# A third of a projection's K as seven block products in an attention and two-stage gated kernel on one core

## The chip, the core and the metric

The kernel runs on one core of a Trainium2 chip. The metric is the device time of one execution in microseconds; of several runs the median counts. Five engines work from queues of their own: TensorE (PE; its weight loads are PEld), VectorE (DVE), ScalarE (ACT), GpSimd (POOL) and SyncE (SP). SP issues most of the transfers and GpSimd some.

## What is computed

Everything is float32. A windowed attention gives x, 2304 tokens by 512; x goes through a gated stage and a projection, and the result through a second gated stage without the nonlinearity, w3 and a last projection.

```python
attn_out = softmax_window_64(q, k, v)           # (4, 8, 576, 64)
x = attn_out.transpose(0, 2, 1, 3).reshape(2304, 512)
# first stage, w_gate and w_val (512, 1536), w_out (1536, 512)
g = x @ w_gate
h = (g * (1.0 / (1.0 + np.exp(-g)))) * (x @ w_val)
x2 = h @ w_out
# second stage, w1 and w2 (512, 1024), w3 (1024, 1024), w_out2 (1024, 512)
return ((x2 @ w1) * (x2 @ w2) @ w3) @ w_out2
```

## The kernel before

A float32 matrix product is done in words: each operand is split into a high word of reduced precision (a cast, L218, mostly on ScalarE) and a rest (the operand less its high word, L227, on VectorE), and three matmuls (high by high, high by rest, rest by high) make one product. A block product of 256 by 256 by 384 tokens is six matmuls where it has two slabs of K.

*Tiling.* The 2304 tokens lie in thirds (`tp`) of 768, each in two halves of 384 (`T`). The inner dimension of the first stage has six blocks `fp` of 256.

*Gated stages* (`gated`, matmuls at L687). A unit is one `fp`, one of the two matrices (`x` is 0 for w_gate, 1 for w_val) and one third. Its two-by-two block product is made as seven block products of six matmuls each (numbered 1 to 7; two slots of a unit's time grid belong to its neighbours). They go into four PSUM banks al, ga, be, de (with an a or b behind, for x 0 or 1). Product 1 goes to al; ScalarE copies al out (c11, L377), product 2 goes to ga, and VectorE adds ga to the copy (L699). `AT` is the grid: 1, 2, 5, 6, then those of other units between, 7, 4, 3. VectorE multiplies the two matrices' results to h (`put`, L709), and h goes to DRAM as two stores for each `fp` and third (L777), from SP's queue in the first stage and from GpSimd's in the second. 36 units make the first stage, 24 the second. In the last `fp` of the first stage the order of units was w_gate over all thirds, then w_val over all thirds.

*Projection* (`project`, L852). It takes a third of the tokens at a time. For each of 12 K slabs and 8 output banks (4 output blocks by 2 halves) three matmuls run: 864 in all. h comes back from DRAM by `Rows` (L811, one key being one `fp` and one half, 384 KB, named pl; ph is its high word). The words of w_out lie in 16 tiles of six 128 by 128 blocks (`Resident`, L1306), loaded from DRAM where `Split` put them earlier. The eight banks are copied out to X at the end of a third (L838 and the lines of copies).

*Preparing weights.* Blocks of weights are loaded into staging tiles st_* by SP (L263), turned into words on VectorE and ScalarE (L194 to L227) and, for w_out, w_out2 (z) and w3, written to DRAM (L1238, L1241). w3 is transposed on VectorE in 32 by 32 pieces into one of two tiles by_w (L1225), and each half of a block leaves by four stores of 32x16x32 elements (L1245), 64 in all, in runs of 128 bytes, from SP.

*What sets the order.* A planner in Python (`Plan`) puts the jobs of VectorE, ScalarE, GpSimd and the queues between the matmuls, by rank and due time, with estimated costs, free slots (`NSLOT` 56 tiles of 384 KB) and a count kept back (`keep`). `plan.need` forces a job that a matmul needs. Events at a unit or at a step of the projection start the making of weights and the loads. An SP transfer also waits for the one eight before it, since they share eight semaphores.

Of the kernel before, what the change touches and what calls it, by code (L numbers as in the profile page):

```python
# [35 lines left out]

@with_exitstack
def window_attention_moe_kernel(ctx: ExitStack, tc: tile.TileContext, q, k, v, w_gate, w_val, w_out, w1, w2, w3, w_out2, out):
# [13 lines left out]
    NSLOT = 56  # L52
# [5 lines left out]
    half = ctx.enter_context(tc.tile_pool(name="half", bufs=7))  # L58
# [27 lines left out]
    class Job:  # L86
        def __init__(self, fn, after=(), cost=None, lag=0.0, rank=0, slots=0, due=0.0, early=False):

            self.rank, self.slots, self.due, self.early = rank, slots, due, early
            self.fn, self.after, self.cost, self.lag, self.done = fn, [x for x in after if x], cost, lag, None  # L90

    class Plan:
        def __init__(self):
# [4 lines left out]

            self.slots, self.keep = NSLOT - ATTENTION, 0

        def job(self, fn, after=(), lag=LAG, slots=0, due=0.0, early=False, **cost):
            j = Job(fn, after, cost, lag, self.rank, slots, due, early)
# [14 lines left out]
        def emit(self, j, e):  # L117
# [4 lines left out]
            j.done = self.free[e] + j.lag  # L122

# [5 lines left out]
        def fill(self, but):  # L129
            limit = self.now + self.ahead  # L130
            while True:
                best = None
                for e, free in self.free.items():
# [3 lines left out]
                    for j in self.queue:  # L137
                        if e not in j.cost or (j.early and e == "DVE" and not self.early) or any(x.done is None for x in j.after):
                            continue
                        if j.slots and self.slots < j.slots + self.keep:  # L140
# [44 lines left out]
    def narrow(part, load, due):  # L185
# [7 lines left out]
        n = 512  # L193
# [17 lines left out]
    def cast(hi, src, after, n, slots=1, negate=False, due=0.0):  # L211
# [7 lines left out]
        return plan.job(fn, after, slots=slots, due=due, early=True, ACT=act(n), DVE=0.1 + 0.0006 * n,  # L219
# [18 lines left out]
    def loading(fn, after=(), slots=0, lag=9.0):  # L238
        return plan.job(fn, after, lag=lag, slots=slots, SP=0.5)
# [4 lines left out]
    class Doubles:  # L244
# [5 lines left out]
        def load(self):  # L250
# [13 lines left out]
            if self.second is None:  # L264
                self.loaded = [loading(lambda eng: part(eng, 0, 2), before, lag=plan.landing)] * 2
            else:
# [4 lines left out]
        def narrowed(self):  # L271
            return [narrow(lambda j=j: self.st[:, 512 * j:512 * j + 512], self.loaded[j], self.due) for j in range(2)]
# [4 lines left out]
    class Weights(Doubles):  # L277
# [3 lines left out]
        def __init__(self, w, n, name):  # L281
            super().__init__(w[:, 256 * n:256 * n + 256].rearrange("(c p) f -> p c f", p=P), name)
            self.ops, self.jobs, self.count, self.gone = {}, {}, 0, 0
# [13 lines left out]
        def make(self):  # L297
# [7 lines left out]
            for p in PRODUCTS:  # L305
                after, due = ready if p in sums else [ready[at[p][1] - 1]], self.due + AT[p]
# [346 lines left out]

    def gated(xop, left, order, func, hd, events, apart=0):
# [20 lines left out]
        class Unit:  # L675
# [26 lines left out]
            def put(self, i, t, src):  # L702

                h, direct = self.h(i, t), (i, t) == (1, 0)
                if self.x and direct:
# [8 lines left out]
                elif direct:  # L714
                    negated(h, src)
# [754 lines left out]
```

## Time and profile before

| | us |
|---|---|
| median of 3 runs | 824.29 |
| lowest and highest | 823.33 and 826.74 |
| the profiled execution | 825.91 |
| its span, by the profile | 824.2 |
| PE busy in it | 815.6 |
| projection, from its first matmul to its last | 149.99 |

The profile comes from one execution. Its engines' busy times and its timelines are in microseconds from the span's start; a row of a timeline has the start, the duration, the engine and line, the operation, and in brackets the idle time before it with what ended it. Two matmuls overlap, so a row of one says 0.33 while the next starts 0.17 later. Stages lie so: attention to about 107, first gated stage to 363, projection 363.35 to 513.34, second gated stage, w3 and the last projection.

### The profile page before, as it was taken

The numbers are of one execution on the slowest core, as the hardware profiler recorded it, in microseconds if no ns is written. First come the engines' busy times: TensorE is split into PE (matmuls) and PEld (weight loads), VectorE is DVE, ScalarE is ACT, GpSimd is POOL, SyncE is SP. The second block draws the span as 40 slices with busy tenths as digits, with TensorE's granted clock in tenths as the row PEclk, the third lists the DMA queues.
The fourth block names the chain that finished last, engine by engine and source line by source line (L and its number), as shares of the span: only waits on it lengthen the run. The fifth ranks groups of instructions, "written<-read, shape, count | busy, mean of one in ns | idle before, by whom it ended". The sixth has DMA issues, their size and how long they took to land.

```text
span 824.2 us, 15599 instructions
## 1 busy us (share of the span) xinstructions
PE 815.6 (99%) x5718; PEld 785.2 (95%) x5718; DVE 640.6 (78%) x1354; ACT 454.6 (55%) x1194; POOL 92.4 (11%) x135
## 2 busy tenths in 40 slices
PE   9999999999999999999999999999999999999998
PEld 6777899999999999999999999999999998899997
DVE  5999889686887939865888683877888844789994
ACT  7899987555555535633564551444444423755543
POOL 3666833000000000000000000000010100000000
PEclk9999999999999999999999999999999999999999
DMA  9989396253562344599996722024555289007632
GB/s 187 199 186 199 61 217 125 90 192 128 192 229 83 137 153 161 210 360 380 385 290 157 233 71 103 20 83 142 167 180 175 110 299 335 27 2 207 181 73 78
DMA packets 172766, 140.23 MB, mean 170 GB/s; under 512 B 120849, under 2 KB 142609, under 8 KB 171665
## 3 DMA queue, kind: packets, MB, share of 16 engines
q1 hardware_dynamic: 167888, 125.86, 50.8%
q0 software_dynamic: 4800, 13.37, 5.9%
q8 instruction: 45, 0.74, 0.4%
q14 instruction: 33, 0.26, 0.1%
HBM read 92.27 MB, written 42.99 MB: 164 GB/s over the span
## 4 chain that ended last, share of the span: by engine, by line
PE 90%; SPq 4%; DMA 2%; ACT 1%; DVE 1%; issue 1%; ACTq 0%
PE o L852 18%; PE ala L687 15%; PE alb L687 14%; PE bea L687 7%; PE beb L687 7%; PE acc L1010 5%; PE al L1153 4%; PE gaa L687 4%; PE gab L687 3%; SPq L403 2%; PE be L1153 2%; PE al L1085 2%; PE PV L519 2%; PE PT L499 2%; PE S L466 1%; PE T L429 1%
## 5 line engine op out<-in xcount | busy, mean ns | idle before, releaser
L852 PE MATMUL o<-ph,wo 128*128 128x384 f32 x576 | 146.4, 334 | 0.0
L852 PEld LDWEIGHTS o<-ph,wo 128*128 128x128 f32 x576 | 104.1, 188 | 0.0
L852 PE MATMUL o<-pl,wo 128*128 128x384 f32 x288 | 96.3, 334 | 0.0
L377 ACT ACTIVATE ha<-ala 128x384 f32<-128x384 f32 x102 | 49.6, 488 | 50.0 <-PE ala L687 49.3
L777 POOL DMA_DIRECT2D h<-ha x24 | 13.0, 546 | 548.2 <-DVE ha L709 548.2
L699 DVE TENSOR_TENSOR ha<-ha,bea 128x384 f32<-128x384 f32 x60 | 33.2, 553 | 38.3 <-PE bea L687 22.3
L852 PEld LDWEIGHTS o<-pl,wo 128*128 128x128 f32 x288 | 54.1, 188 | 0.3 <-DVE pl L227 0.3
L480 ACT ACTIVATE pexp<-S,stat 128x128 f32<-128x128 f32 x144 | 53.1, 421 | 0.0
L218 ACT CAST hf<-h 128x384 fp32r<-128x384 f32 x84 | 38.8, 513 | 14.5 <-DVE h L231 13.2
L712 ACT ACTIVATE ha<-ha 128x384 f32<-128x384 f32 x54 | 28.4, 526 | 33.1 <-DVE ha L699 33.1
L227 DVE TENSOR_TENSOR hf<-h,hf 128x384 fp32r<-128x384 f32 x84 | 42.3, 548 | 4.8 <-ACT hf L218 4.8
L227 DVE TENSOR_TENSOR pl<-pl,ph 128x768 fp32r<-128x768 f32 x36 | 33.4, 953 | 14.6 <-ACT ph L218 14.3
L218 ACT CAST ph<-pl 128x768 fp32r<-128x768 f32 x36 | 29.1, 839 | 26.2 <-DMA pl<-h 23.6
L490 POOL TENSOR_TENSOR pexp<-pexp,stat 128x384 f32<-128x384 f32 x48 | 39.1, 835 | 28.6 <-DVE stat L487 14.1
L377 ACT ACTIVATE c12b<-alb 128x384 f32<-128x384 f32 x30 | 14.8, 492 | 48.7 <-PE alb L687 48.6
L480 ACT ACTIVATION_READ_ACCUMULATOR pexp<-S,stat 128x1 f32 x144 | 37.2, 260 | 0.0
L699 DVE TENSOR_TENSOR c22b<-c22b,beb 128x384 f32<-128x384 f32 x30 | 16.6, 553 | 25.8 <-ACT c22b L377 25.8
L687 PE MATMUL ala<-xo,w_g_7h 128*128 128x384 f32 x120 | 30.4, 336 | 0.5 <-ACT ha L377 0.5
L687 PE MATMUL ala<-xo,w_g_1h 128*128 128x384 f32 x126 | 29.2, 335 | 0.0
L473 DVE TENSOR_REDUCE stat<-S 128x3 f32<-128x384 f32 x48 | 24.4, 550 | 4.8 <-PE S L466 4.4
L218 ACT CAST xp<-X 128x384 fp32r<-128x384 f32 x42 | 19.7, 520 | 10.5 <-DVE X L231 7.5
L377 ACT ACTIVATE c11b<-alb 128x384 f32<-128x384 f32 x30 | 14.7, 490 | 19.2 <-PE alb L687 19.2
(628 smaller groups left out, 2465.8 us busy)
## 6 DMA issues: line engine op xcount, KB each, us to landing
h<-ha SPq DMA_DIRECT2D x36, 384.0 KB, 3.0
pl<-h SPq DMA_DIRECT2D x36, 384.0 KB, 6.1
h<-ha POOLq DMA_DIRECT2D x24, 384.0 KB, 3.2
h<-h SPq DMA_DIRECT2D x24, 384.0 KB, 6.7
st_w<-in_moe_w_dram SPq DMA_DIRECT2D x8, 1024.0 KB, 6.2
st_wo<-in_moe_w_out_dram SPq DMA_DIRECT2D x6, 1024.0 KB, 5.5
wo<-by_wo SPq DMA_DIRECT2D x12, 512.0 KB, 4.0
st_g<-in_moe_w_gate_dram SPq DMA_DIRECT2D x5, 1024.0 KB, 6.4
```

Of the source, the lines that this page charges most:

```text
L218: (eng.copy if eng is nc.scalar else eng.tensor_copy)(out=hi(), in_=src())
L227: return plan.job(lambda eng: eng.tensor_tensor(out=lo(), in0=src(), in1=hi().bitcast(F32), op=ALU.subtract), after, slots=slots, due=due, ...
L377: nc.scalar.mul(out=out, in_=in_, mul=-1.0)
L473: nc.vector.tensor_reduce(out=st[:, 0, x, :], in_=sc[2 * m + x], op=ALU.max, axis=AX.X, negate=True)
L480: nc.scalar.activation(out=pe[:, jj, :], in_=so[:, jj, :], func=AF.Exp, bias=st[:, 0, x, jj:jj + 1], accum_out=st[:, 1, x, jj:jj + 1])
L490: nc.gpsimd.tensor_tensor(out=pe, in0=pe, in1=st[:, 3, x, :].unsqueeze(2).to_broadcast([P, SUB, P]), op=ALU.mult)
L687: nc.tensor.matmul(acc, lhsT=self.wt.ops[p, x][:, m, :], rhs=self.xs.ops[p, m][:, y, :], start=start and n == 0, stop=n == 5, skip_group_c ...
L699: nc.vector.tensor_tensor(out=out, in0=x, in1=y, op=ALU.add)
L712: nc.scalar.activation(out=h, in_=src, func=func, scale=-1.0 if direct else 1.0)
L852: nc.tensor.matmul(acc[m, x], lhsT=wos.tiles[i // 6][:, i % 6, :], rhs=rows[2 * tp + x].words(f, b), start=f == n == 0, stop=f == NF - 1 a ...
L1010: nc.tensor.matmul(acc, lhsT=w3T[i][c // 3][:, x, (c % 3) * P:(c % 3) * P + P], rhs=zt[c, y], start=c == k == 0, stop=c == NI - 1 and k == 2)
L1153: nc.tensor.matmul(acc, lhsT=right.ops[p, m, y][:, P * k:P * k + P], rhs=self.xs.ops[p, m][:, x, :], start=bool(name) and n == 0, stop=n = ...
```

## The change

*Seven products.* In the projection the blocks `fp` 0 and 1 (`SEVEN`, a third of K) are taken as two-by-two block products: halves of tokens by halves of the slab pairs, in seven products over both, in the order of `STEPS`. Each product runs for two output blocks m and two g (the two `fp`). Bank al is copied by ScalarE into ga (after product 1) and into de (after product 7), and later products accumulate there. The four other blocks are plain as before, but go bank by bank (al, be, ga, de). Evictions become copies and additions into X.

*Its operands.* h of these blocks is stored in the layout `h7d`, as seven parts (four transfers for two, 1.75 times the bytes), and twelve transfers from DRAM to DRAM with an addition, on GpSimd's queue, make the sums (`spread`). w_out's blocks 0 and 1 are made by class `Seven`: four sums and seven rests of 256 columns, stored in 14 pieces. Row keys per third go from 12 to 15, w_out's tiles from 16 to 20. Rows have slots of their own (`ROWS`).

*Seeded units.* From unit 6 on in both gated stages ScalarE copies al into bank ga, and product 2 accumulates on it. Product 2 changes places with product 5 (`AT_SEEDED`). VectorE's addition of ga is gone.

*Others.* The stores of w3 go by GpSimd's queue. The last `fp` of the first stage runs in the order that the second had (thirds first). Staging loads of w_out and w3 are made with the weights, with a due time; loads of w_out's tiles hang on events. `NSLOT` is 58, `half` has 5 buffers.

```diff
+AT_SEEDED = {1: 0, 5: 2, 2: 3, 6: 4, 7: 8, 4: 12, 3: 13}
-    NSLOT = 56
+    NSLOT = 58
-    half = ctx.enter_context(tc.tile_pool(name="half", bufs=7))
+    half = ctx.enter_context(tc.tile_pool(name="half", bufs=5))
...
+    SEEDED = 6
+    SEVEN = (0, 1)
...
+                elif (i, t) == (0, 0) and self.seeded:
+                    nc.scalar.copy(out=h, in_=src)
+                    plan.charge("ACT", act(T))
...
+                    self.seeded = self.n >= SEEDED
+                    if self.seeded:
+                        self.ga = bank(f"ga{self.name}")[:, :T]
+                    self.c11 = self.ga if self.seeded else self.own(0, 0, "c11")
                     later(1, lambda: self.copy(self.c11, self.al))
+                elif p == 2 and self.seeded:
+                    plan.wait(self.read)
+                    self.mm(self.ga, 2)
+                    self.put(0, 0, self.ga)
...
+    H_AT = {1: 0, 7: 1, 2: 2, 3: 3, 4: 4, 6: 5, 5: 6}
+    def spread(fp, tp, h):
+        to, f = h7d[tp], SEVEN.index(fp)
+        (h0, h1) = (t.rearrange("p (c t) -> p c t", c=2) for t in h)
+        for at, src in (((0, 2), h0), ((2, 4), h1), ((4, 6), h1), ((6, 7), h0[:, :1])):
+            nc.sync.dma_start(out=to[:, at[0]:at[1], f, :], in_=src)
...
+            def add(p, by, after):
+                j = plan.job(lambda eng: eng.dma_start(out=to[:, H_AT[p]], in_=to[:, H_AT[by]], accum_op=ALU.add),
+                             [done, *after], lag=8.0, DMA=1.0)
+                stored[p, tp, 7] = [j]
+                return j
+            s5 = add(5, 7, [])
+            add(7, 3, [s5])
+            s6 = add(6, 5, [s5])
+            add(4, 6, [s6])
...
+    STEPS = (1, 5, 6, 2, 7, 3, 4)
...
+            def seed(to, src, m, name):
+                open_bank(to, m, name)
+                nc.scalar.copy(out=to[m], in_=src[m])
...
+            for k, p in enumerate(STEPS):
...
+                to = {2: ga, 5: be, 3: be}.get(p, al)
+                for m in range(2):
+                    if p in (1, 5):
+                        open_bank(to, m, "al" if p == 1 else "be")
+                    for g in range(2):
+                        product(to[m], (p, 7), p, g, m, p in (1, 5) and g == 0, True)
+                    if p == 1:
+                        seed(ga, al, m, "ga")
+                    elif p == 5:
+                        copy(1, 1, be, m)
+                    elif p == 6:
+                        copy(0, 1, al, m)
+                    elif p == 7:
+                        seed(de, al, m, "de")
...
+            for k, fp in enumerate(plain):
...
+                for g in range(2):
+                    last = g == 1 and fp == plain[-1]
+                    for b, (i, c, to) in enumerate(((1, 0, al), (0, 1, be), (0, 0, ga), (1, 1, de))):
+                        for m in range(2):
+                            product(to[m], (fp, c), (fp, i), g, m, False, last)
...
-                by.append(plan.job(lambda eng, j=j, t=t: self.put(eng, self.n, j, t[0]), [a], lag=6.0, SP=2.0))
+                by.append(plan.job(lambda eng, j=j, t=t: self.put(eng, self.n, j, t[0]), [a], lag=7.0, DMA=4.0))
...
-    order1 = unit_order(NF2, [(x, tp) for x in range(2) for tp in range(NTP)])
-    order2 = unit_order(NI2, [(0, 0), (0, 1), (1, 0), (1, 1), (0, 2), (1, 2)])
+    ENDS = [(0, 0), (0, 1), (1, 0), (1, 1), (0, 2), (1, 2)]
+    order1, order2 = unit_order(NF2, ENDS), unit_order(NI2, ENDS)
```

The order of instructions, at the three places that matter here. TensorE at a place where one unit (alb, gab, beb, w_v) begins between the products of another (ala, w_g); xo are the operands from x. Before:

```order
L687 MATMUL alb_0_3340<-xo_10_781,w_v_1h 128x384 x3
L687 MATMUL alb_0_3340<-xo_11_798,w_v_1h 128x384 x3
L687 MATMUL ala_2_3283<-xo_70_2578,w_g_7h 128x384 x2
L687 MATMUL ala_2_3283<-xo_70_2578,w_g_6l 128x384
L687 MATMUL ala_2_3283<-xo_71_2581,w_g_7h 128x384 x2
L687 MATMUL ala_2_3283<-xo_71_2581,w_g_6l 128x384
L687 MATMUL gab_0_3364<-xo_20_1049,w_v_1h 128x384 x2
L687 MATMUL gab_0_3364<-xo_20_1049,w_v_4h 128x384
L687 MATMUL beb_0_3376<-xo_50_1305,w_v_4h 128x384 x2
L687 MATMUL beb_0_3376<-xo_50_1305,w_v_7h 128x384
```

The same place after:

```order
L699 MATMUL alb_0_3409<-xo_10_791,w_v_1h 128x384 x3
L699 MATMUL alb_0_3409<-xo_11_808,w_v_1h 128x384 x3
L699 MATMUL ala_2_3329<-xo_70_2590,w_g_6h 128x384 x2
L699 MATMUL ala_2_3329<-xo_70_2590,w_g_6l 128x384
L699 MATMUL ala_2_3329<-xo_71_2593,w_g_6h 128x384 x2
L699 MATMUL ala_2_3329<-xo_71_2593,w_g_6l 128x384
L699 MATMUL beb_0_3435<-xo_50_1315,w_v_4h 128x384 x2
L699 MATMUL beb_0_3435<-xo_50_1315,w_v_4l 128x384
L699 MATMUL gab_0_3416<-xo_20_1059,w_v_1h 128x384 x2
L699 MATMUL gab_0_3416<-xo_20_1059,w_v_4h 128x384
```

Product 5 (beb) stands ahead of product 2 (gab), so that another product and product 5 lie between product 1 and product 2.

SyncE at the start of the projection, between the stores of the last h (h_2_92) and the row keys behind them. A name like pl_0_3 before is half 0 of block 3; wo_114 and the like are the words of w_out in DRAM. Before:

```order
L1306 DMA wo_4915<-wo_116 128x256
L1306 DMA wo_4918<-wo_116 128x768
L777 DMA h_2_92<-ha_2_0_4583 128x768
L777 DMA h_2_92<-ha_2_1_4584 128x768
L811 DMA pl_0_3_5019<-h_0_84 128x2x384
L811 DMA pl_1_3_5021<-h_0_84 128x2x384
L1241 DMA zd_117<-by_z_0_5031 128x1024
```

After, where pl_2_1 is half 1 of block 2 (the second plain key of the first third; the seven-product keys and pl_2_0 stand ahead of the stores):

```order
L1487 DMA wo_4899<-wo_120 128x768
L805 DMA h_2_92<-ha_2_0_4793 128x768
L805 DMA h_2_92<-ha_2_1_4794 128x768
L1487 DMA wo_4994<-wo_121 128x768
L1487 DMA wo_4996<-wo_121 128x256
L1487 DMA wo_4996<-wo_122 128x512
L1487 DMA wo_5000<-wo_122 128x512
L1487 DMA wo_5000<-wo_123 128x256
L875 DMA pl_2_1_5015<-h_0_81 128x2x384
L875 DMA pl_3_0_5034<-h_0_84 128x2x384
```

The key of the first plain block stands behind the last stores of h and three more tiles of w_out; before, half of the blocks' keys stood ahead of them.

VectorE at the end of the projection's second third, where w3 is transposed (by_w) ahead of X's evictions. Before:

```order
L1225 STREAM_TRANSPOSE by_w_0_5840<-st_w_5701 128x512
L207 SCALAR_TENSOR_TENSOR st_w_5701<-st_w_5701 128x512
L1225 STREAM_TRANSPOSE by_w_1_5848<-st_w_5701 128x512
L838 TENSOR_SCALAR X_1_0_5412<-o_0_0_5416 128x384
L838 TENSOR_SCALAR X_1_1_5413<-o_1_0_5418 128x384
```

After:

```order
L1388 STREAM_TRANSPOSE by_w_1_5876<-st_w_5656 128x512
L214 SCALAR_TENSOR_TENSOR st_a_5768<-st_a_5768 128x512
L915 TENSOR_TENSOR X_1_0_5460<-X_1_0_5460,be_0_5493 128x384
L915 TENSOR_TENSOR X_1_1_5461<-X_1_1_5461,be_1_5504 128x384
L214 SCALAR_TENSOR_TENSOR st_a_5768<-st_a_5768 128x512
```

The transpose still stands ahead of the evictions, which are now additions from the banks be; the stores that empty by_w have moved to GpSimd's queue.

## Rows read from the trace of the kernel before

**Rows 1.** The page: busy time of each engine; the clock granted in 40 slices.

```profile
PE 815.6 (99%) x5718; PEld 785.2 (95%) x5718; DVE 640.6 (78%) x1354; ACT 454.6 (55%) x1194; POOL 92.4 (11%) x135
...
PEclk9999999999999999999999999999999999999999
```

**Rows 2.** Waits of TensorE: total us, times, longest.

```profile
PE on L548 <- DVE still L542: 1.1, 1, 1.1
...
PE alb L687 <- ACT c22b L377: 0.8, 1, 0.8
...
PE al L1085 <- DVE hf L227: 0.4, 1, 0.4
```

**Rows 3.** The chain that ended last: start, length, what.

```profile
349.83 2.08 PE alb L687 x12
...
363.35 149.99 PE o L852 x864
```

**Rows 4.** Timeline of TensorE, first gated stage.

```profile
294.13 0.33 PE L687 MATMUL alb<-xo,w_v_1l 128*128 128x384 f32 x1
...
296.38 0.51 PE L687 MATMUL beb<-xo,w_v_1l 128*128 128x384 f32 x2
...
313.07 0.34 PE L687 MATMUL alb<-xo,w_v_7l 128*128 128x384 f32 x1
314.20 0.62 PE L687 MATMUL alb<-xo,w_v_1h 128*128 128x384 f32 x2 [0.80 <-ACT c22b L377]
```

**Rows 5.** Timeline of VectorE, where st_g is late.

```profile
308.31 0.77 DVE L194 TENSOR_SCALAR st_g<-st_g 128x512 int32<-128x512 int32 x2 [2.77 <-DMA st_g<-in_moe_w_gate_dram]
```

**Rows 6.** Timeline of SyncE's queue, around the projection's start.

```profile
354.16 0.79 SPq L777 DMA_DIRECT2D h<-ha  x2
...
380.38 1.20 SPq L811 DMA_DIRECT2D pl<-h  x2
```

**Rows 7.** Windows: us, busy of PE, PEld, DVE, ACT, POOL; PEclk, DMA share, GB/s.

```profile
180.00:240.00 60.00, 60.00 (x348) 60.00 (x347) 48.18 (x104) 31.56 (x69) 0.00 (x0) 1.00 0.46 166
340.00:345.00 5.00, 5.00 (x31) 5.00 (x30) 4.56 (x10) 3.65 (x9) 0.00 (x0) 1.00 0.14 15
345.00:415.00 70.00, 70.00 (x404) 69.73 (x404) 47.73 (x77) 30.86 (x52) 0.00 (x0) 1.00 1.01 378
355.00:360.00 5.00, 5.00 (x31) 5.00 (x30) 4.05 (x7) 2.44 (x4) 0.00 (x0) 1.00 0.97 341
463.30:513.30 50.00, 50.00 (x290) 50.00 (x289) 35.22 (x71) 23.78 (x46) 0.00 (x0) 1.00 0.34 120
600.00:640.00 40.00, 40.00 (x233) 40.00 (x232) 35.09 (x73) 18.44 (x41) 2.29 (x5) 1.00 0.63 191
```

**Rows 8.** Timeline of ScalarE, casts of the late row keys.

```profile
386.06 0.83 ACT L218 CAST ph<-pl 128x768 fp32r<-128x768 f32 x1 [6.57 <-DMA pl<-h]
387.08 0.84 ACT L218 CAST ph<-pl 128x768 fp32r<-128x768 f32 x1 [0.18 <-DMA pl<-h]
```

**Rows 9.** The page's groups: busy, mean ns of one, idle before; rests and casts.

```profile
L227 DVE TENSOR_TENSOR pl<-pl,ph 128x768 fp32r<-128x768 f32 x36 | 33.4, 953 | 14.6 <-ACT ph L218 14.3
L218 ACT CAST ph<-pl 128x768 fp32r<-128x768 f32 x36 | 29.1, 839 | 26.2 <-DMA pl<-h 23.6
```

**Rows 10.** Timeline of ScalarE, the copy of alb in the unit of rows 4.

```profile
294.50 0.49 ACT L377 ACTIVATE c11b<-alb 128x384 f32<-128x384 f32 x1
```

**Rows 11.** Tile w3d: issues of its stores, and their landing.

```profile
L1245 SPq DMA_DIRECT2D w3d<-by_w x64: 303/492/1932, 413.5 to 629.5; - x64
...
DMA to landing us min/median/max: 1.7/2.7/9.2
```

**Rows 12.** Groups by line of GpSimd: transfers that it issues.

```profile
L777 POOL DMA_DIRECT2D h<-ha x24 | 13.0, 546 | 548.2 <-DVE ha L709 548.2
...
L236 POOL DMA_DIRECT2D xo<-X x10 | 10.1, 1112 | 11.0 <-ACT xo L359 11.0
...
L236 POOL DMA_DIRECT2D X<-X x10 | 10.0, 1183 | 4.2 <-DVE w_v_4l L227 3.3 <-DVE st_g L194 0.6 <-DVE xo L227 0.2
```

More of the change, by code (lines that the diff above doesn't have):

```diff
@@ L209, in narrow, with cast @@
                         [c], due=due, DVE=dve(n))
[L211 removed]
+    def cast(hi, src, after, n, slots=1, negate=False, due=0.0, rows=0):
         def fn(eng):
@@ new lines, in hi, with words @@
+                return self.hi[key]
+            a = loading(load, stored[key[0], self.tp, 7] if key[1] == 7 else stored[key[0], self.tp], rows=1, lag=9.0, due=due)
+            b = cast(hi, lambda: self.lo[key].bitcast(F32), [a], 2 * T, 0, rows=2, due=due)
+            (a.behind, b.behind), Rows.before = Rows.before, (a, b)
+            self.jobs[key] = rest(lambda: self.lo[key], lambda: self.lo[key].bitcast(F32), lambda: self.hi[key], [b], 2 * T, due=due)
+        def words(self, key, g, x):
+            return (self.lo if x else self.hi)[key][:, g, :]
@@ new lines, in project, with open_bank, part, copy @@
+            al, ga, be, de = ([None] * 2 for _ in range(4))
+            r = rows[tp]
+            def open_bank(to, m, name):
+                to[m] = bank(f"{name}{tp}_{m}")[:, :T]
+            def seed(to, src, m, name):
+                open_bank(to, m, name)
+                nc.scalar.copy(out=to[m], in_=src[m])
+                plan.charge("ACT", act(T))
+            def part(r, c, m):
+                return x2[2 * r + m][:, T * c:T * c + T]
+            def copy(r, c, src, m):
+                (negated if r == c else nc.scalar.copy)(out=part(r, c, m), in_=src[m])
+                plan.charge("ACT", act(T))
@@ new lines, in add, with product @@
+            def add(r, c, src, op, m):
+                nc.vector.tensor_tensor(out=part(r, c, m), in0=part(r, c, m), in1=src[m], op=op)
+                plan.charge("DVE", dve(T))
+            def product(acc, key, w, g, m, start=False, stop=False):
+                plan.need(r.jobs[key])
+                for n, (x, y) in enumerate(PASSES):
+                    plan.need(wos.job(w, g, x, m))
+                    nc.tensor.matmul(acc, lhsT=wos.words(w, g, x, m), rhs=r.words(key, g, y),
+                                     start=start and n == 0, stop=stop and n == 2, skip_group_check=not start)
@@ L1314, in project_loads, with job, words, used @@
+        def job(self, w, g, x, m):
+            return self.jobs[self.col(w, g, x, m) // 768]
+        def words(self, w, g, x, m):
+            s, c = divmod(self.col(w, g, x, m), 768)
+            return self.tiles[s][:, c // P]
+        def used(self, k):
+            plan.slots += 4 * (k + 1) // 3 - 4 * k // 3
+    def project_loads(tp):
         keep, plan.rank = plan.rank, -1
-        for f in pairs:
+        rows[tp] = Rows(tp)
+        for k, p in enumerate(STEPS):
+            rows[tp].queue((p, 7), 100 * tp + k)
+        for k, fp in enumerate([fp for fp in range(NF2) if fp not in SEVEN]):
```

284 lines of the change are left out of this document (185 added, 99 removed).

## The prediction

> **What bounds the kernel now.** I read the page first: TensorE is busy 99% of the span, at the full granted clock in every slice, and VectorE 78% [rows 1]. Then its waits: the longest inside the matrix stages is 0.8 us on alb at L687; the others of note lie in the attention, ahead of the change's reach [rows 2]. Then the chain that ended last: the whole projection stands in it as one piece of PE, 864 matmuls in 149.99 us [rows 3]. That is 173.6 ns a matmul, as in the last pieces of the gate (12 in 2.08 us). So TensorE's instruction count sets the time, and another engine or a transfer matters only where it makes a matmul wait. The working is on the profiled run: 825.91 us (span 824.2), 1.62 above the median of 824.29. I work out changes to the 825.9 and take 1.6 off.
>
> **The change part by part.**
>
> *Seven products.* A third of K, four block products per quarter as eight, becomes seven: 84 matmuls instead of 96 for each third of the tokens, 36 fewer in all. The order confirms 36, and the count of no other TensorE stage changes. 36 x 173.6 ns = **-6.25 us**, all on the path.
>
> *The pause at 313.* Between the pieces at 313.07 and 314.20 PE loses 1.0 us (the listed 0.8, and the slowed pieces around it) [rows 4]. Its releaser is the copy c22b, late because VectorE stood 2.77 us for the words of st_g, which landed at 308.3 [rows 5]. The change makes staging blocks of w_out and w3 together with the weights and moves this load about one unit (7.28 us) earlier; what would be late next, the xo additions, is long done there. **-1.0 us**, between 0 and -1.0.
>
> *Row keys in the first third.* The plain row blocks come behind all the seven-product operands, and SP issues in order. SP held before until 354.16, when VectorE had finished the last store's half h_0_90 [rows 6]; the new order of units ends that part one unit earlier, so at 354.16 - 7.28 = 346.9. From there to pl_2_1, the second key of the first plain block, SP issues 28 transfers of 384 KB (0.393 MB): three pairs of h stores, 13 tiles of w_out, 9 row keys, 11.0 MB. The queues are the limit: over 345 to 415 us their share is 1.01 at 378 GB/s, though 341 in 355 to 360, where stores and tiles mix [rows 7]. At 378: 29.1 us, so 376.0. The same sum before: 30 such transfers and 3.15 MB of staging and stores, 14.95 MB from 345.0, would end at 384.6; the casts of that pair began at 386.06 and 387.08 [rows 8]; I add 2.0 us. Then cast 0.84 and rest 0.95 [rows 9], 0.2 for hand-over: ready at 380.0. PE starts the projection at 363.35 and wants pl_2_1 after seven steps of 12 matmuls (14.58) and one key (1.04), at 379.0. **+1.05 us**; at 341 GB/s it is 32.3 us and +4.3; with no lag it is nothing. I take the mean rate, as this stretch has the same mix as the 70 us. The pause of 1.0 moves PE's need and SP's release alike if it goes. Behind it the reserve grows: a plain block (2 keys and 2.7 tiles, 1.8 MB, 4.9 us) feeds 48 matmuls (8.3 us).
>
> Here a page speaks: the Trainium skill, page "DMA: Bandwidth & Descriptors", section "Where 436 GB/s comes from", says that transfers between HBM and SBUF are held to about 358 GB/s per core. The trace disagrees: 378 over 70 us [rows 7]. By the page the sum would be 30.7 us and the wait about 2.7 us, an estimate.
>
> *Other work of the projection.* 45 casts and rests instead of 36 add 7.6 and 8.6 us to ScalarE and VectorE, and 24 more seeds and evictions of about 0.49 us go mostly to ScalarE. Cover: in the last 50 us VectorE is busy 35.2 and ScalarE 23.8 [rows 7], and a third of the addition is at most 7 us on each. If the cover fails at the end (xp operands for the second gate), I see 0.2 to 0.3 us.
>
> *Sums of h in DRAM, and the seven words of w_out.* 12 additions of 0.393 MB, and 3.5 MB more of h stores, fall between about 180 and 240 us, where DMA share is 0.46 [rows 7], over 100 us before they are read: nothing. Were that cover gone, SP's loads there would shift by microseconds, with 19 us in hand at the next weights. VectorE's 3.2 us more for each w_out block lie in the same stretch, busy 48.2 of 60 [rows 7]: nothing.
>
> *Seeded units.* From unit 6 of either gate ScalarE copies al into bank ga, and product 2 accumulates on it, moved behind product 5. This takes 48 additions (26 us) off VectorE, which buys no TensorE time, and puts a copy between two matmuls. Unit with alb and gab: p1's last matmul starts at 294.13, p2 would now start 1.04 (a foreign product) and 1.04 (p5) later at 296.38 [rows 4]; the copy runs 294.50 to 294.99 [rows 10], 1.4 us early. It slips when ScalarE or VectorE's queue is behind; over the units of the trace, two others have under 0.4 us left. Bounds 0 and 1.5 us over all; with xp above I take **+0.5**.
>
> *Stores of w3 by GpSimd's queue.* 64 stores move off SP, where each held the queue for 492 ns and landed in 2.7 us [rows 11]. SP gets 31 us back in places where it isn't late: nothing. On GpSimd no row has this shape: 512 runs of 128 bytes. Its store of ha, 128 runs, takes 546 ns; its accumulating transfers 1112 and 1183 [rows 12]. Bounds for one: 0.55 (a fixed cost) to 2.2 (four times, by runs), at the extreme 4.4 (four times the adds). I take 1.0, nearer to the plain store: like it, nothing is added up. Who waits: the next transposes on VectorE, since there are two by_w buffers, and what stands behind them there, X additions of the projection. Eight transposed tiles fall in the second third, so six must be out before the eighth is written: 412.5 + 24p + 2.5. Here 412.5 is a microsecond before the first issue of these stores, 24 are six tiles of four stores, 2.5 is the landing [rows 11]. At p = 1.0 that is 439, and the adds come at 459 (363.35 and 552 matmuls): hidden. It starts to cost at p = 1.83.
>
> Sum: 825.9 - 6.25 - 1.0 + 1.05 + 0.5 = 820.2; at the median, 1.6 less, **818.6**.
>
> **The rivals.**
>
> *B, bytes late.* The first third runs at 341 to 358 GB/s, or the later seven-product tiles are late too. For: the 15 GB/s in 340 to 345, so nothing is fetched ahead, and the 341 of the mixed stretch [rows 7]. Against: 378 over the whole. Wait 2.7 to 4.3, with a second key or tile late 1 to 2 more: 820 to 824.
>
> *C, GpSimd's stores hold VectorE (slower).* Place: by_w_1's last transpose in the second third, ahead of the X additions that free the be banks; PE's product 5 of the last third needs one at 461.2 (two steps into it). Price, with 1.1 for two additions: 412.5 + 24p + 2.5 + 1.1 - 461.2. At p = 2.2 it is 7.7 us (826.5); it ends above 824.3 from p = 2.1, and at 4.4 it is 60 us. For: 128-byte runs, four times as many. Against: 546 ns rows, and eight of the 16 tiles only.
>
> On this the Trainium skill, page "SBUF — State Buffer", section "SBUF: two separate sides", says that descriptors of a GpSimd-queue DMA can't be written while VectorE holds the shared port; its next section has a DMA of 620 ns become 3100 ns. This speaks against the change. The trace disagrees for the shape it has: the ha stores took 546 ns on average [rows 12] where VectorE was busy 35 of 40 us [rows 7]. By the page p would be 3.1 and the time about 848, an estimate.
>
> *D, seeds bind.* Copies slip behind other ScalarE work, so that product 2 waits 0.1 to 0.2 us in 48 units: +5 to +10, so 823 to 828. For: the listed pause was such a copy. Against: 1.4 us typical slack.
>
> *E, the change doesn't remove the work.* Excluded: 36 matmuls are gone.
>
> **How the numbers follow.** A measurement of this kernel tells 0.5% from no change, 4.1 us: faster is below 820.2, slower above 828.4. Forecast A, small waits (816.8 to 821): 0.60, of which 0.52 faster. B 0.18 (0.03 faster, 0.15 same). C 0.10 (0.08 slower, 0.02 same). D 0.08 (0.07 same, 0.01 slower). The remaining 0.04: other waits gone, 0.03 faster, 0.01 same. So 0.58 faster, 0.33 same, 0.09 slower. Low end: no wait at all is 825.9 - 6.25 - 1.0 - 1.6 = 817.05, with a quarter of a microsecond for short pauses like that at L1085 [rows 2] 816.8. High end: B's worst and D's lower half, 825.0. Outside: C above it and D's tail, some 0.15, and a little below.
>
> **What would show it.** L-line groups of the projection with 828 matmuls in 143.7 us plus waits; a wait on pl (from L227's rest) near 379, 0 to 2 us; no c22b wait near 313; w3d issues on POOL under 1.8 us each; VectorE without idle on by_w; product 2 waits on ACT under 0.5 us in sum. I am wrong if PE's waits in 379 to 400 exceed 4 us, if be waits near 461, or if matmuls take other than 173.6 ns.

## The result, and the profile after

The changed kernel takes 834.53 us (median of 4 runs, 832.83 to 838.18) where the kernel before takes 824.22: ratio 1.0126, interval 1.0085 to 1.0168. It is slower by 10.3 us; forecast was 818.6, with 825.0 as the upper end. The profiled executions are 838.18 us (span 836.5) of after and 825.91 (span 824.2) of before, so the rows below add up to 12.3 us, 2 more than the medians differ by.

Where TensorE stands at the matmul of the same number in both programs, counted from the first of the gated stage (us from the span's start; the last column is the delay that came in since the line above):

| | before | after | grown by |
|---|---|---|---|
| first gated stage begins | 94.3 | 95.9 | 1.6 |
| its matmul 505 | 187.2 | 189.8 | 1.0 |
| its matmul 883 | 252.7 | 268.9 | 13.6 |
| projection begins | 363.35 | 379.6 | 0.1 |
| projection ends | 513.3 | 524.7 | -4.9 |
| span | 824.2 | 836.5 | 0.9 |

The projection gives nearly what was forecast. The time is lost in the first gated stage, between 187 and 269. TensorE's waits of after (total, times, longest), against [rows 2]:

```profile
PE bea L699 <- DVE ha L711: 3.8, 1, 3.8
PE gaa L699 <- ACT gaa L385: 3.8, 2, 2.0
...
PE alb L699 <- ACT c22b L385: 1.1, 1, 1.1
...
PE al L922 <- ACT X L911: 0.9, 1, 0.9
```

The first two lines are three waits, which end at 199.85, 222.21 and 245.34. The chain that ended last says what is behind them (start, length, what); it no longer stays on PE there:

```profile
186.39 10.32 DMA st_v<-in_moe_w_val_dram
...
212.78 17.45 DMA w<-by_wo
...
233.01 9.63 DMA st_wo<-in_moe_w_out_dram
...
245.34 1.31 PE gaa L699 x6
```

VectorE's timeline at these loads (in brackets the idle time before):

```profile
196.73 0.77 DVE L201 TENSOR_SCALAR st_v<-st_v 128x512 int32<-128x512 int32 x2 [2.82 <-DMA st_v<-in_moe_w_val_dram]
...
219.72 0.77 DVE L201 TENSOR_SCALAR st_g<-st_g 128x512 int32<-128x512 int32 x2 [6.51 <-DMA st_g<-in_moe_w_gate_dram]
220.40 1.29 DVE L204 SCALAR_TENSOR_TENSOR st_g<-st_g 128x512 int32<-128x512 int32 x2
221.60 0.55 DVE L711 TENSOR_TENSOR ha<-ha,bea 128x384 f32<-128x384 f32 x1
...
242.67 0.43 DVE L201 TENSOR_SCALAR st_wo<-st_wo 128x512 int32<-128x512 int32 x1 [4.74 <-DMA st_wo<-in_moe_w_out_dram]
```

and SyncE's queue, which issued them:

```profile
186.39 0.49 SPq L270 DMA_DIRECT2D st_v<-in_moe_w_val_dram  x1
188.08 15.32 SPq L840 DMA_DIRECT2D h<-ha  x8
...
207.11 0.37 SPq L270 DMA_DIRECT2D st_g<-in_moe_w_gate_dram  x1
211.10 21.86 SPq L1369 DMA_DIRECT2D w<-by_wo  x7
233.01 0.43 SPq L270 DMA_DIRECT2D st_wo<-in_moe_w_out_dram  x1
```

These staging loads take 9.7 to 12.6 us from issue to first use, and VectorE stands before them. Its queue is in order: at the second wait the addition of bea to ha, which TensorE waits for, stands behind the first words of st_g. At the first and the third wait it is ScalarE's copy into gaa that is late, since it stands behind the scaling of the same load's words, which waits for VectorE. ScalarE's timeline at the first:

```profile
198.13 1.29 ACT L210 ACTIVATE st_v<-st_v 128x512 f32<-128x512 f32 x2 [3.78 <-DVE st_v L204]
199.33 0.47 ACT L385 ACTIVATE gaa<-ala 128x384 f32<-128x384 f32 x1
```

The seven stores of a w_out block (w<-by_wo, 211 to 233) wait for words that VectorE makes behind st_g, and the next staging load, at 233.01, stands behind them on SyncE, so one late load delays the next. In the kernel before the same loads were used 7 to 18 us after their issue, with no idle time, for instance:

```profile
170.46 0.61 SPq L263 DMA_DIRECT2D st_v<-in_moe_w_val_dram  x1
...
210.06 0.38 SPq L263 DMA_DIRECT2D st_g<-in_moe_w_gate_dram  x1
```
```profile
188.72 0.76 DVE L194 TENSOR_SCALAR st_v<-st_v 128x512 int32<-128x512 int32 x2
...
217.05 0.76 DVE L194 TENSOR_SCALAR st_g<-st_g 128x512 int32<-128x512 int32 x2
```

The same 63 products' stretch in windows of before and after (us, busy of PE, PEld, DVE, ACT, POOL, then PEclk, DMA share, GB/s), first before:

```profile
187.20:252.70 65.50, 65.50 (x380) 65.50 (x378) 52.93 (x114) 38.50 (x84) 0.00 (x0) 1.00 0.47 167
```
```profile
189.80:268.90 79.10, 70.70 (x381) 68.03 (x380) 51.59 (x114) 38.12 (x88) 9.08 (x11) 0.96 0.84 246
...
222.00:226.00 4.00, 3.70 (x12) 3.19 (x12) 2.72 (x7) 3.05 (x7) 0.81 (x1) 0.61 1.08 251
248.00:250.00 2.00, 2.00 (x8) 2.00 (x7) 1.97 (x5) 0.66 (x2) 0.00 (x0) 0.50 0.08 22
```

The queues' share goes from 0.47 to 0.84. Of the 13.6 us, 8.4 are time without a matmul (79.10 less 70.70). Some 3.4 are matmuls at the lower of TensorE's two clock levels (1.2 GHz, 0.50 in the row) after the second and the third pause, 1.7 each time by the granted clock of the rows around them. The other 1.8 lie at the pauses: nothing overlaps the last matmul before one, and the second behind it starts some 0.28 us after the first instead of 0.17.

### The profile page after: what moved, and what is told of

Its sections match the earlier page's. It is cut to its first block, busy times and chain, and to the rows that moved or that the text cites. A ratio compares the mean times of both kernels' runs of the same rounds, so it can differ in the third digit from the quotient of the medians.

```text
span 836.5 us, 15712 instructions
## 1 busy us (share of the span) xinstructions
PE 815.5 (97%) x5682; PEld 781.2 (93%) x5682; DVE 630.0 (75%) x1337; ACT 474.0 (57%) x1242; POOL 143.4 (17%) x211
## 4 chain that ended last, share of the span: by engine, by line
PE 77%; DMA 10%; SPq 4%; DVE 4%; ACT 2%; issue 2%; POOL 0%; ACTq 0%; DVEq 0%; POOLq 0%
PE ala L699 13%; PE alb L699 11%; PE bea L699 6%; PE beb L699 6%; PE acc L1119 5%; PE al L922 5%; PE al L1262 4%; PE be L922 3%; PE gaa L699 3%; PE gab L699 3%; DMA pl<-h 3%; PE ga L922 3%; SPq L411 2%; DMA w<-by_wo 2%; PE be L1262 2%
## 5 line engine op out<-in xcount | busy, mean ns | idle before, releaser
L1410 POOL DMA_DIRECT2D w3d<-by_w x64 | 41.5, 656 | 264.7 <-DVE by_w L1388 263.6
L922 PE MATMUL al<-ph,wo 128*128 128x384 f32 x192 | 54.2, 335 | 0.9 <-ACT X L911 0.9
L385 ACT ACTIVATE ha<-ala 128x384 f32<-128x384 f32 x78 | 38.2, 489 | 26.6 <-PE ala L699 26.4
L234 DVE TENSOR_TENSOR pl<-pl,ph 128x768 fp32r<-128x768 f32 x45 | 41.9, 952 | 10.3 <-ACT ph L225 9.8
L225 ACT CAST hf<-h 128x384 fp32r<-128x384 f32 x84 | 38.4, 514 | 13.8 <-DVE h L238 13.6
L922 PE MATMUL be<-ph,wo 128*128 128x384 f32 x144 | 41.4, 334 | 0.0
L922 PEld LDWEIGHTS al<-ph,wo 128*128 128x128 f32 x192 | 35.2, 188 | 1.2 <-ACT X L911 1.2
L922 PE MATMUL ga<-ph,wo 128*128 128x384 f32 x120 | 34.8, 334 | 0.0
L922 PE MATMUL al<-pl,wo 128*128 128x384 f32 x96 | 32.1, 334 | 0.0
L922 PE MATMUL de<-ph,wo 128*128 128x384 f32 x96 | 28.2, 334 | 0.0
L699 PE MATMUL alb<-xo,w_v_7h 128*128 128x384 f32 x114 | 27.6, 336 | 0.4 <-ACT c12b L385 0.4
```

Source lines behind the costliest of these rows:

```text
L225: (eng.copy if eng is nc.scalar else eng.tensor_copy)(out=hi(), in_=src())
L234: return plan.job(lambda eng: eng.tensor_tensor(out=lo(), in0=src(), in1=hi().bitcast(F32), op=ALU.subtract), after, slots=slots, due=due, ...
L385: nc.scalar.mul(out=out, in_=in_, mul=-1.0)
L699: nc.tensor.matmul(acc, lhsT=self.wt.ops[p, x][:, m, :], rhs=self.xs.ops[p, m][:, y, :], start=start and n == 0, stop=n == 5, skip_group_c ...
L922: nc.tensor.matmul(acc, lhsT=wos.words(w, g, x, m), rhs=r.words(key, g, y), start=start and n == 0, stop=stop and n == 2, skip_group_check ...
L1410: eng.dma_start(out=w3d[512 * j:512 * j + 512, P * i + 32 * a:P * i + 32 * a + 32].rearrange("(b p) f -> p b f", p=32), in_=t[32 * a:32 * ...
```

## The experiments

The forecast put the sums of h at nothing. First their price, then what makes it. The expectations speak of four theories. Theory 1: the additions fill the queues, so that staging loads land late. Theory 2: the extra stores of h hold SyncE's queue. Theory 3: making w_out's blocks together with the weights puts the loads in a bad order. Theory 4: the additions only stretch the landing of a load, and that costs because the changed order issues the loads too shortly before their use.

### Without the additions, and additions alone

```diff
-                j = plan.job(lambda eng: eng.dma_start(out=to[:, H_AT[p]], in_=to[:, H_AT[by]], accum_op=ALU.add),
-                             [done, *after], lag=8.0, DMA=1.0)
+                j = done
```

> The changed kernel without the twelve additions (four of the seven operands of h are then not the sums). Theory 1: 821 to 825, the price of the additions in full. Theory 2: 832 to 836. Theory 3: 831 to 836.

825.9 us (ratio 1.0027, 1.0008 to 1.0046), just above theory 1's range. The stretch from matmul 505 to 883 takes 66.8 us: the loss there is gone but for 1.3. The additions cost 8.6 us in this kernel by the medians (8.2 by the two ratios). The three loads of the waits in both runs (landing in us from issue; an addition counts as beside a load when both are in flight at some time):

| load, issued in after at | lands in after | additions beside it | lands without additions |
|---|---|---|---|
| st_v, 186.39 | 10.3 | 1 | 8.1 |
| st_g, 207.11 | 12.6 | 9 | 5.2 |
| st_wo, 233.01 | 9.6 | 1 | 7.2 |

So the largest wait stands beside nine additions, the two others beside one. The load st_g without additions (SyncE and VectorE; no idle time before it):

```profile
202.46 0.37 SPq L270 DMA_DIRECT2D st_g<-in_moe_w_gate_dram  x1
```
```profile
208.48 0.76 DVE L201 TENSOR_SCALAR st_g<-st_g 128x512 int32<-128x512 int32 x2
```

Then the same number of them on the kernel before:

```diff
                             store(out=hd[self.fp, self.tp][:, i, :], in_=t)
                         plan.slots += 2
+                        if func != AF.Copy and self.fp == 1:
+                            a, b = hd[1, self.tp], hd[0, self.tp]
+                            for out, x in ((a[:, 0], b[:, 0]), (a[:, 1], a[:, 0]), (b[:, 1], a[:, 0]), (b[:, 0], b[:, 1])):
...
+                                nc.gpsimd.dma_start(out=out, in_=x, accum_op=ALU.add)
```

> The kernel before, with twelve DRAM-to-DRAM additions of the same size added on GpSimd's queue after the stores of h of block 1 (they add parts of h of blocks 0 and 1 to one another, so h is not the reference's). Theory 1: 830 to 836 from 824.3, with TensorE's waits between 185 and 250 us. Rival (the additions cost only on top of the seven-part stores, which fill the queues first): 824 to 827.

824.5 us (1.0003, 0.9982 to 1.0025): nothing, so theory 1 as it stood falls. The queues were as full as in the changed kernel (share 0.85 from matmul 505 to 883, where after has 0.84):

```profile
190.00:200.00 10.00, 10.00 (x60) 10.00 (x59) 7.54 (x18) 6.75 (x16) 1.66 (x2) 1.00 1.02 278
220.00:230.00 10.00, 10.00 (x60) 10.00 (x59) 9.63 (x22) 4.64 (x12) 1.66 (x2) 1.00 0.99 264
```

but GpSimd issued them at most two at a time, and the tightest load with several of them beside it (three) was 8.1 us old at its use. VectorE idled 1.0 us there, and TensorE not at all (rows of this run, SyncE and VectorE):

```profile
208.28 0.38 SPq L263 DMA_DIRECT2D st_g<-in_moe_w_gate_dram  x1
```
```profile
216.35 0.76 DVE L194 TENSOR_SCALAR st_g<-st_g 128x512 int32<-128x512 int32 x2 [0.98 <-DMA st_g<-in_moe_w_gate_dram]
```

In after, GpSimd issued three additions at 201.87 and three at 209.72, since the stores that they wait for had queued up on SyncE.

### The doubled stores

> As the run without additions, and h of blocks 0 and 1 stored once (two transfers instead of four; the row loads read as many bytes, from the parts that are there). Theory 1: at most 2 us below the run without additions. Theory 2: 822 to 826, where the run without additions stays at 832 to 836. Theory 3: 831 to 836.

823.3 us (0.9977, 0.9956 to 0.9999): 2.6 us below the run without additions, a little more than theory 1 allowed, far from what theory 2 wanted of the stores alone. The stretch from matmul 505 to 883 takes 66.7 us, as in the run without additions. What differs in the profiled runs is the projection, 144.8 us against 148.4, where a pause at its second third is 0.4 us instead of 2.0.

### Where the additions stand

```diff
+                                nc.gpsimd.dma_start(out=gate_d[self.fp, self.tp], in_=hd[self.fp, self.tp][:, 0, :8])
...
-                             [done, *after], lag=8.0, DMA=1.0)
+                             [done, held_adds[tp, p], *after], lag=8.0, DMA=1.0)
```

> The changed kernel with its twelve DRAM-to-DRAM additions held back: on GpSimd's queue each group of them stands behind a small transfer that reads a later stored h (blocks 3 and 4), so they run from about 255 us on instead of 186 to 240. Theory 1 (the additions fill the queues in 185 to 245, so weights land late and VectorE, then TensorE, stand): the three waits of TensorE in 187 to 250 go, the time falls from 834.5 to 822 to 826. Theory 2 (the extra stores of h hold SyncE's queue): 832 to 836, waits stay. Theory 3 (w_out's blocks made together with the weights put the loads in a bad order): 831 to 836.

833.9 us, above theory 1's range. The old stretch is clean (67.0 us), but the time is lost again where the additions now run (272 to 350): with two of them issued at 316.4, VectorE waits for a load issued at 318.05:

```profile
330.96 0.76 DVE L201 TENSOR_SCALAR st_wo<-st_wo 128x512 int32<-128x512 int32 x2 [6.11 <-DMA st_wo<-in_moe_w_out_dram]
```

One by one, held in the same way behind units 14 to 31:

> The changed kernel with its twelve additions held back one by one, each behind a small transfer on GpSimd's queue that waits for a later unit's h (units 14 to 31, from about 200 to 325 us). Theory 4 in the form that several additions at once stretch the landings: 825 to 829. If a single one in flight is enough to make a load late: 831 to 835, as with the additions held back in groups.

830.4 us (1.0084, 1.006 to 1.0108): between the two expectations, 4 us better than in bunches. The median landing of an addition is 6.7 us, against 9.7 in after.

### What stands beside them

```diff
-        coming += [x] + wo[n * len(wo) // len(rest1):(n + 1) * len(wo) // len(rest1)]
+        coming += [x] + [wo[i] for i in (2, 3, 0, 1, 4, 5)[n * len(wo) // len(rest1):(n + 1) * len(wo) // len(rest1)]]
```

> The changed kernel with w_out's blocks made in the order 2, 3, 0, 1, 4, 5, so that the two seven-product blocks are made from about 230 us on, behind most of the additions, which stay at 186 to 240. If the collision of the additions with these blocks (short leads of the staging loads, 14 stores on SyncE) makes the cost: waits between 187 and 250 us under 2 us, 825 to 830. If additions and doubled stores cost by themselves: 832 to 837.

828.6 us (1.006, 1.0042 to 1.0077). The additions run at 185 to 227 as before, without the seven-product blocks of w_out beside them, and the time is 5.9 us lower. One wait is left in that stretch, 3.4 us at 211.8, from a load with nine additions beside it:

```profile
198.03 0.37 SPq L270 DMA_DIRECT2D st_g<-in_moe_w_gate_dram  x1
```
```profile
212.68 0.77 DVE L201 TENSOR_SCALAR st_g<-st_g 128x512 int32<-128x512 int32 x2 [5.46 <-DMA st_g<-in_moe_w_gate_dram]
```

> As the run before it, with the additions held back one by one behind later units (200 to 325 us). If single additions are harmless beside plain blocks but not beside seven-product blocks: above the run before it, 827 to 832. If spreading helps in any order: 822 to 827.

834.0 us (1.0121): spreading moves the additions to 200 to 325, and so onto the seven-product blocks in their new place; waits at 255.9 (3.2), 305.7 to 310.8 (2.8) and 332.6 (2.1). Together: the additions cost most where they meet these blocks. They are not free without them either: with the blocks moved away the stretch from matmul 505 to 883 still takes 71.4 us, 5.8 more than in the kernel before, and the load beside nine additions lands in 14.6.

### How early a load is issued

The short lead by itself, on the kernel before (`ahead=2` becomes 0 in `make_to`), then with the twelve additions:

> The kernel before with loads of weight blocks asked for only when they are made (ahead 0 instead of 2), so that they are issued a few us ahead of their use; no additions. Theory 4: some cost by itself, 825 to 832; it is the base for the next run.

863.7 us, more than expected: the cost lies mostly elsewhere (pauses of 7.9 us from 677.8 and 6.0 from 402.3).

> The same with the twelve additions, which cost nothing on the kernel before (824.5). Theory 4: 4 to 10 us above the short lead without additions. Rival (additions are free wherever the stores are not doubled): within 2 us of it.

869.4 us. The ratios' intervals (1.0427 to 1.0507, and 1.0489 to 1.0566) overlap a little, so the 5.7 us are likely, not certain; the stretch from matmul 505 to 883 has 48.9 us instead of 45.1 for its first two thirds. The load st_v, first without and then with additions (issue on SyncE, use on VectorE):

```profile
198.92 0.42 SPq L263 DMA_DIRECT2D st_v<-in_moe_w_val_dram  x1
```
```profile
205.93 0.77 DVE L194 TENSOR_SCALAR st_v<-st_v 128x512 int32<-128x512 int32 x2 [1.23 <-DMA st_v<-in_moe_w_val_dram]
```
```profile
196.40 0.41 SPq L263 DMA_DIRECT2D st_v<-in_moe_w_val_dram  x1
```
```profile
205.75 0.76 DVE L194 TENSOR_SCALAR st_v<-st_v 128x512 int32<-128x512 int32 x2 [3.74 <-DMA st_v<-in_moe_w_val_dram]
```

The load lands in 7.0 and, with three additions beside it, in 9.3. So it is likely that additions which are free on the kernel before cost once the load is short of time. (The expectation on the third buffer below says that leads before were 13 to 19 us; more than half of those in the first gated stage were 6 to 9.)

Two tries at more lead in the changed kernel failed. Without the lines that make w_out's and w3's blocks with the weights:

> The changed kernel without the lines that make a block of w_out or w3 together with the weights ahead of it; they are made with the next weights, as in the kernel before. Theory 1 and theory 2: 831 to 837, waits in 187 to 250 stay. Theory 3: 822 to 828, and those waits go.

844.9 us: theory 3 had the wrong sign, these lines help. With a third staging buffer (`bufs=3`, `ahead=3`, NSLOT 55):

> The changed kernel, additions and all, with a third staging buffer and each block's load issued one block earlier (NSLOT 55 for the room). Theory 4 (the additions only stretch a load's landing from 6 to 10 to 12 us, and it costs because the changed order issues loads 5 to 12 us ahead of their use, where before it was 13 to 19): waits between 185 and 250 us under 2 us in sum, time 825 to 829. Rival (the queues' volume itself is what costs there): 832 to 836, waits stay.

904.3 us, waits everywhere; the three slots given up, or the earlier loads, cost far more than was at stake. VectorE no longer idles before the staging loads issued between 178 and 307 us (leads of 10 to 34), but TensorE waits for ScalarE's copies instead (gab, 17.4 us in 8 waits), so the time decides nothing on theory 4. On top of it:

> As the run with a third staging buffer, and the planner's landing times are longer: 8 us for the stores of prepared words (5), 12 for the first third's row keys (9), so that casts stand further back on ScalarE. If the waits at the end of the first gated stage (about 1.3 us, copy c22b behind casts of row keys) and at the second third (1 to 2.3 us, copies of al behind casts of w3) come from that order: 2 to 5 us below the run with a third buffer, 821 to 826. If not, the same.

908.0 us, nothing gained.

### Sums on GpSimd

```diff
+                nc.gpsimd.tensor_tensor(out=x, in0=x, in1=y, op=ALU.add)
+                part[p] = x
+            for p in (5, 7, 6, 4):
+                nc.gpsimd.dma_start(out=to[:, H_AT[p], f, :], in_=part[p])
```

> The changed kernel with the sums of h made by GpSimd in SBUF (24 additions of 128x384 in place, then the seven parts stored once each, the four sums from GpSimd's queue) instead of the twelve DRAM-to-DRAM additions; as many bytes go to DRAM by plain stores as before them. Theory 1 (the additions as transfers are what costs): 824 to 828, near the 825.9 of the run without additions. Rival (any way of making the sums costs as much, by the smaller stores or by GpSimd's work beside VectorE): 830 to 835.

834.5 us (1.0108): the rival's time. Waits of 4.0 us in all between 138 and 162 and 5.1 between 196 and 211, where the additions run and VectorE is nearly full, first this run, then after:

```profile
138.00:162.00 24.00, 20.65 (x113) 19.21 (x112) 22.02 (x42) 13.47 (x32) 11.64 (x15) 1.00 0.40 135
```
```profile
138.00:162.00 24.00, 24.00 (x140) 24.00 (x140) 19.64 (x46) 15.01 (x36) 0.00 (x0) 1.00 0.52 184
```

42 instructions took VectorE 22.0 us, where 46 others took 19.6. By shape, the same additions of two SBUF operands in that window, first this run (those of st_v, which meet GpSimd's additions of 153.5 to 158.3; those of st_g, which don't), then after:

```profile
L238 DVE TENSOR_TENSOR st_v<-st_v 128x256 f32<-128x256 f32 x4 | 3.3, 824 | 0.0
...
L238 DVE TENSOR_TENSOR st_g<-st_g 128x256 f32<-128x256 f32 x4 | 1.7, 413 | 0.0
```
```profile
L238 DVE TENSOR_TENSOR st_v<-st_v 128x256 f32<-128x256 f32 x4 | 1.7, 421 | 0.0
```

On this the Trainium skill, page "SBUF — State Buffer", section "SBUF: two separate sides", says that VectorE and GpSimd share a pair of ports as an exclusive lock, which an instruction of VectorE with two SBUF inputs needs beside one of GpSimd that reads SBUF. These rows agree with that: 824 ns beside GpSimd's additions, 413 and 421 without them.

### Seeds, w3's stores, and everything else

> As the run without additions (825.9), and no unit of the gated stages is seeded: VectorE adds ga again and product 2 stands ahead of product 5. The prediction's term (seeds cost some 0.5 us): 825 to 826. Seeds that bind in 48 units: 816 to 821. Seeds that help, since VectorE is late in many places: 827 to 835.

832.4 us (1.0086, 1.0066 to 1.0106) against 825.9: the seeds gain 6.5 us in the kernel without additions. Without them VectorE has 48 additions more, and row keys and the second stage's weights come late:

```profile
382.69 0.45 PE L921 MATMUL be<-ph,wo 128*128 128x384 f32 x1 [3.29 <-ACT ph L225]
...
659.07 1.43 PE L699 MATMUL alb<-xp,w_b_1h 128*128 128x384 f32 x6 [1.70 <-ACT w_b_1h L225]
```

> As the run without additions (825.9), with the stores of w3 on SyncE's queue again. The prediction's term (hidden on GpSimd, and SyncE not late where they stood): 825 to 827. Stores that hold VectorE on GpSimd: 819 to 824. SyncE late with the row keys when it has to issue them: 828 to 834.

825.6 us (1.0005) against 825.9: the queue of these stores makes no difference, as forecast.

> The changed kernel with all six blocks of the projection plain: 864 matmuls, no seven-part stores, no additions, w_out's blocks by the old class; seeds, order of units, staging with the weights and w3's stores on GpSimd's queue stay. If what the seven products need (additions, doubled stores, 15 row keys, 20 tiles) takes their 6.25 us and more: 819 to 824, at or below the kernel before. If the rest of the change (short leads of the staging loads, seeds) costs: 828 to 836.

826.3 us (1.0025, 1.0008 to 1.0042), two above the kernel before and out of the first case by as much: the rest of the change gains nothing by itself. Its one large pause in the matrix stages is that of c22b at the end of the first stage, 1.8 us.

### Two joined versions

On the run with the additions one by one:

> As the run before it, and the blocks of w_out2 and w3 are made from step 5 of the projection on instead of step 0, and the planner takes the first third's row keys as landing after 12 us (9). If the waits at the end of the first stage and at the second third come from casts that stand ahead of ScalarE's copies: 2 to 5 us below the run before it. If not: the same or above.

829.4 us (1.0062), 1 us below the run with additions one by one: within the intervals. On the run with the seven-product blocks later and the additions one by one:

> As the run before it, with w_out2 and w3 made from step 5 of the projection on and the first third's row keys taken as landing after 12 us. Candidate for a kernel below both: 820 to 824 if the terms add, else as the run before it.

834.3 us (1.0124): no better than its base. None of the versions that compute the whole result beats the kernel before; the nearest are the one without seven products (826.3) and, with them, the one with their blocks of w_out later (828.6).

## Why the prediction was wrong, by its own steps

*Seven products, -6.25: right.* 36 matmuls are gone, and the projection is 4.9 us shorter in the profiled runs, with 1.3 us of waits in it.

*The pause at 313, -1.0: right.* No gap over 0.15 us stands between 250 and 375 in after.

*Row keys, +1.05: mechanism right, size small.* The wait at the second plain key is 0.2 us, at 395.1, where 379.0 plus the delay of 16.3 puts it (0.8 in the run without additions). The queues ran at 385 GB/s from 363 to 413; rival B didn't come.

*Sums of h in DRAM, nothing: the step that failed.* It took the mean share of the queues, 0.46 in [rows 7], and 100 us of time until the sums are read. Both are true and neither is the point. What counts is the other transfers: how long a staging load takes beside the additions, against how long it has until VectorE, in order, reaches its first word. The prediction spoke of 19 us in hand at the next weights. That was the long end: of the loads issued between 160 and 260 us in the kernel before, four were used 17 to 19 us after their issue and four 7 to 9. In after VectorE idled 2.8 to 6.5 us in front of three of them. The reserve was gone before the additions came: in the run without them the loads issued between 180 and 230 us are used 6 to 9 us after their issue. The doubled stores didn't take it (with single stores it is 6 to 9 too). The runs point to the seven-product blocks of w_out, which the prediction put at nothing in the same step: where they are made later, or not at all, the load of st_v issued at 162 to 164 us is used 22 us later. The runs put the term of the additions at 8.6 us. In the profiled run 3.4 of the stretch's 13.6 are the lower clock after the pauses; the four runs of after have mean granted clocks of 0.994, 0.998, 0.999 and 0.994 at 838.2, 832.8, 833.7 and 835.4 us, so the median carries only a part of that.

Of the prediction's signs one failed: product 2 was to wait on ScalarE under 0.5 us in sum, and two of the three waits, 3.8 us, are product 2 waiting for ScalarE's seed copy into gaa. That is rival D's way of losing time, in two units and not in 48. The seeds aren't its cause by themselves: without the additions these two waits are gone. The three signs that it named for being wrong didn't come: TensorE's waits behind the start of the projection stay far under 4 us, there are no be waits at the start of its last third, and its matmuls keep their pace. The stage where the time was lost was not among them.

*The doubled stores, nothing: 2.6 us.* They don't act where the additions do (66.7 and 66.8 us from matmul 505 to 883). In the profiled runs the difference lies in the projection; how the stores come to bear there isn't shown.

*Seeds, +0.5 with xp: wrong sign.* "Buys no TensorE time" read VectorE's load as slack, while the new row keys and the second stage's weights were about to need it. Measured: -6.5, in the kernel without additions.

*Other work of the projection, 0.2 to 0.3: short.* A copy c22b stands behind casts of row keys on ScalarE at the end of the first stage (1.3 us), and the copies of al behind a word of w3 at the second third (1.05 in after, 2.2 in the run without additions, and there the lower clock as well). ScalarE of after, the second place:

```profile
427.59 0.70 ACT L210 ACTIVATE st_w<-st_w 128x512 f32<-128x512 f32 x1 [2.44 <-DVE st_w L204]
428.17 0.86 ACT L911 COPY X<-al 128x384 f32<-128x384 f32 x2
```

*GpSimd's stores: right.* Estimate 1.0 us each, measured 0.66 (page of after; busy, mean ns of one):

```profile
L1410 POOL DMA_DIRECT2D w3d<-by_w x64 | 41.5, 656 | 264.7 <-DVE by_w L1388 263.6
...
L805 POOL DMA_DIRECT2D h<-ha x24 | 13.2, 552 | 152.0 <-DVE ha L721 151.9
```

Rival C didn't come. The Trainium skill's rule on VectorE and descriptors (page "SBUF — State Buffer", section "SBUF: two separate sides"), with the 3100 ns of its next section, would have made it 3.1 us, an estimate; these rows disagree with that for the instructions that VectorE ran beside these stores.

What stays open: without additions and extra stores the kernel is at 823.3, not 817. Its waits account for some 3 us of that; the rest may lie within what single runs differ by in the attention (first gated stage at 93.0 to 97.1 us in runs that share its code). Nor is it settled how much of the 8.6 us belongs to each of the three things that meet; taking one of them away gives 4.1 (spacing), 5.9 (w_out's blocks elsewhere) or 8.6 (the additions). No run has the additions without the seeds. And no run tells why a load lands so late beside the additions: the queues' share there is as high as in the projection (1.08 in 222 to 226, 1.03 in 363 to 413), but at 251 GB/s instead of 385.

## What to carry to other kernels

Where a queue is free on average, ask for each transfer that an in-order engine waits for how long before its use it is issued and what else is in flight then; a mean share over 60 us hides it. A change that adds traffic and reorders the issuing queue must be costed as a pair: the same additions were free on the old order and cost 8.6 us on the new one. And spare time of an engine that is not the bottleneck is worth something as soon as the same change adds work to it.

## What the runs showed of the chip that was not expected

TensorE's clock after a pause: in the run without additions a pause of 2.0 us at 413.7 was followed by matmuls at the lower level, 0.70, 0.50 and 0.95 in the rows from 416 to 422, some 1.7 us lost; in after a pause of the same length at 197.8 was not (1.00 in 200 to 202), while a shorter one, 1.8 us at 243.6, was (0.50 in 248 to 250 above). What TensorE did before them differs, and no run separates it:

```profile
416.00:418.00 2.00, 2.00 (x10) 2.00 (x10) 2.00 (x5) 2.00 (x6) 0.00 (x0) 0.70 0.94 388
418.00:420.00 2.00, 2.00 (x8) 2.00 (x7) 2.00 (x4) 1.62 (x4) 0.85 (x2) 0.50 1.03 394
420.00:422.00 2.00, 2.00 (x13) 2.00 (x12) 2.00 (x5) 0.72 (x2) 2.00 (x4) 0.95 1.05 250
```
```profile
200.00:202.00 2.00, 2.00 (x12) 1.91 (x12) 1.97 (x4) 0.54 (x2) 0.13 (x1) 1.00 0.16 58
```

A store of 512 runs of 128 bytes costs GpSimd 656 ns, one of 128 runs 552: four times the runs, a fifth more time.
